# One core: six row tiles in one run per weight step of the first token group, and part of the third group's low parts on GpSimd

## The chip, the cores and the metric

The kernel runs on one core of a Trainium2 chip. The metric is the device time of one execution in microseconds (us), taken as the median of several executions. TensorE multiplies (PE in the profile; its weight loads are PEld), VectorE (DVE) and ScalarE (ACT) do elementwise work and read the matmul banks in PSUM, GpSimd (POOL) does elementwise work between SBUF tiles, and SyncE (SP) issues the DMAs.

## The reference, cut to what matters

Attention produces 2304 rows of 512 values; two expert layers follow. The change lies in the second, where every one of 8 experts multiplies all rows, and a gate `P` weighs the results:

```python
def _moe2_ref(x, w_gate, w1, w2):            # x: 2304 x 512
    P = np.exp(x @ w_gate - max)             # 2304 x 8
    for _ in range(8):
        P /= P.sum(1, keepdims=True) + 1e-09
        P /= P.sum(0, keepdims=True) + 1e-09
        P *= N / E
    out = np.zeros((N, D))
    for e in range(E):                       # 8 experts
        h = np.maximum(x @ w1[e], 0.0)       # 512 -> 1024
        ye = h @ w2[e]                       # 1024 -> 512
        out += P[:, e:e + 1] * ye
    return out
```

## The kernel before, in words

**Groups and steps.** The second expert layer takes the rows in three groups of 768, 768 and 640 (`g` = 0, 1, 2), and for each group the weights in 32 steps (`U2`; a step is 256 of an expert's 1024 hidden columns). Step `s` belongs to group `s // 32`. Every float32 operand is split into a high part, rounded for TensorE's fast float32 form, and a low part, the rest; a product is the three matmuls high x low, high x high and low x high.

**The first product of a step** (`quad`, line 908) multiplies 2 x 2 blocks by Winograd's scheme with seven block products `m1`, `m6`, `m5`, `m7`, `m2`, `m4`, `m3`, each six matmuls of 384 columns (320 in the third group), written to three banks `px`, `py` and `pz`. `m1` fills `px`, which ACT copies out as `p1`, and `m2` later adds to the same bank. `m6` fills `py`; DVE adds `p1` into `u2`; `m7` adds to `py`; DVE makes `u3` of it; `m4` adds to `py` again, and DVE makes `c21`. `m5` fills `pz`; with `u3` DVE makes `c22`; `m3` adds to `pz`, and with `u2` DVE makes `c12`. A product that adds to a bank waits until the reader of the bank's earlier state is through. ACT's rectified copies of `c11` (which is `px`), `c21`, `c22` and `c12` are the high parts `g2h`, and DVE makes the low parts `g2l` (line 975), which the list `later` puts off by a place or more.

**The second product of a step** is done, for group 0, one step later by `layer2_moe` (line 1267): six row tiles of 128 rows, each six matmuls of 512 columns into a bank `po` (three banks), which DVE adds, weighed by the gate, to `oa` (line 1303; an eviction below). For groups 1 and 2 it is seven products `pm` of the same scheme, six matmuls each, interleaved with those of the next step, and DVE adds each to `m` (line 1135).

**The order of the work** is written by hand. `experts()` goes through the steps and through seven places `i` of each step; at a place it issues the block product `mults[i]` and then, in group 0, the row tile `t` with `min(t + 1, 6) == i`. After each of them `slot()` lets every lane go one step on: lane `w` splits the next step's first weights (`weights_a`), `w2` this step's second weights (`weights_b`: ACT makes `w2h` as soon as the load `rw` has landed, GpSimd then `w2l`), and `sb` makes the sums of second weights which groups 1 and 2 will use (`sums_b`: two ACT copies and a cast, four DVE sums, two DVE low parts `wz`), stores them and starts the load of the next second weights. In six steps (`APART_AT`) lane `sb` makes a second set of sums, and in four (`SPREAD_AT`) it turns gate weights with TensorE transposes (`spread_p`). All engines run their instructions in the order in which they are written.

**Between groups** the right operands of the next group are made: `sums_of` and `form_now` (line 692) for the third group, where ACT makes a form's high part and DVE its low part in two halves, `T1`, `T3`, `B21`, `T4` and `B22` during steps 63 and 64 (lane `late`).

Of the kernel before, what the change touches and what calls it, by code (L numbers as in the profile page):

```python
# [84 lines left out]
def body(ctx: ExitStack, tc: tile.TileContext, xt_in, xn_in, stb, stk, wd, ws, alpha, wgate, out):  # L85
# [610 lines left out]
    def form_now(g, name, tag, src):  # L696

        t = big.tile([P, 2, 2, CH[2 * g][1]], F32R, tag=tag, name=f"r{name}_{g}")
        right[name, g] = t
        nc.scalar.activation(out=t[:, 0], in_=src, func=AF.Copy)  # L700
        yield 2
        for k in range(2):
            nc.vector.tensor_tensor(out=t[:, 1, k], in0=src[:, k], in1=f32(t[:, 0, k]), op=ALU.subtract)
            yield 1
# [222 lines left out]
    def quad(s):  # L927
# [81 lines left out]

        return [m1, m6, m5, m7, m2, m4, m3]  # L1010

# [336 lines left out]
    def slot():  # L1348
        tick()
        for lane in lanes:  # L1350
            if at_point.get(lane):
                continue
# [104 lines left out]

    APART_AT = [8, 11, 14, 16, 18, 20]
    SPREAD_AT = {22: (1, 0), 23: (1, 3), 24: (2, 0), 25: (2, 3)}

    def experts():
# [3 lines left out]
        for s in range(NS2 + 1):  # L1465
# [24 lines left out]

            lag = 3 if s == 1 else 1

            for i in range(7):
# [4 lines left out]
                if mults:  # L1498
                    point()
                    mults[i]()  # L1500
                    if made:
                        forms_in(made, after[i])
                    if i == 2 and s == 2 * U2 - 1:
                        lanes["late"].append(forms_late(2, after[2:]))
                    if i == 1:
                        while later:
                            later.pop(0)()
                    slot()
                for t in plain:
                    if min(t + lag, 6) == i:  # L1510
                        point()
                        layer2_moe(s - 1, t)
                        if t == 0 and UE < s < U2 - 1:
                            lanes["sb"].append(sums_own(s))
                            if s in APART_AT:
                                lanes["sb"].append(sums_apart(APART_AT.index(s)))
                            if s in SPREAD_AT:
                                lanes["sb"].append(spread_p(*SPREAD_AT[s]))
                        while later and i > 1:
                            later.pop(0)()  # L1520
                        slot()
                if U2 < s < NS2:
                    product(s - 1, i)
                    slot()
            for lane in ("w", "w2", "sums", "blocks"):
                flush(lane)
        flush("out")
        finish_last(NG - 1)
# [66 lines left out]
```

## Time and profile before

| | |
|---|---|
| median of 3 executions | 1772.21 us (1770.85 to 1772.26) |
| the profiled execution's own time | 1771.78 us |
| its span, first to last instruction | 1770.0 us |
| PE busy | 1751.9 us (99%) |
| DVE, ACT, POOL busy | 1418.4, 731.2, 1209.9 us |
| TensorE clock granted in the span | 0.999 of full speed |

The span is the stretch that the trace covers; the execution's own time is 1.78 us longer. PE's busy time counts a matmul from its start to a modelled end, and matmuls overlap, so the useful number for PE is the distance from one start to the next. Times in rows count from the span's start. The second expert layer's steps begin at 379.11 us; in group 0, step 20 begins at 698.65, step 28 at 825.07; step 64, the first of the third group, begins at 1354.80.

### The profile page before, as it was taken

What the parts mean: (1) busy time and instruction counts of PE and PEld (TensorE: products, weight loads), DVE (VectorE), ACT (ScalarE), POOL (GpSimd) and SP (SyncE); (2) the same over time, 40 slices, a digit from 0 to 9 for tenths busy, and PEclk for the clock granted to TensorE, in tenths of its full rate; (3) what the DMA queues carried; (4) which work ended last, traced back from release to release, by engine and by line L of the source; (5) the groups of instructions that cost most, each with busy time, mean ns of one, the idle gap of its engine ahead of it and who ended that gap; (6) DMA issues with size and microseconds to landing.
All of it is one profiled execution on the core that took longest, in us unless ns stands there. A gap on an engine that the chain in (4) does not pass through costs nothing.

```text
span 1770.0 us, 28923 instructions
## 1 busy us (share of the span) xinstructions
PE 1751.9 (99%) x9963; PEld 1635.7 (92%) x9963; DVE 1418.4 (80%) x2356; ACT 731.2 (41%) x1382; POOL 1209.9 (68%) x1288
## 2 busy tenths in 40 slices
PE   8999999999999999999999999999999999999998
PEld 8888888878888888888899999999999999999998
DVE  7879878788977788778877777777898777777877
ACT  7747757553344444444422222222233333322222
POOL 4536546577576766667657777777787897777775
PEclk9999999999999999999999999999999999999999
DMA  6212111227689999888876776777676887888884
GB/s 221 84 54 72 37 60 49 78 79 250 228 316 346 332 341 359 330 309 295 318 289 259 259 262 255 259 261 261 256 259 255 315 296 287 337 311 306 302 313 156
DMA packets 153010, 427.19 MB, mean 241 GB/s; under 512 B 17296, under 2 KB 34192, under 8 KB 152864
## 3 DMA queue, kind: packets, MB, share of 16 engines
q1 hardware_dynamic: 152864, 425.34, 66.4%
q8 instruction: 80, 1.31, 0.3%
q14 instruction: 66, 0.54, 0.1%
HBM read 302.28 MB, written 122.99 MB: 240 GB/s over the span
## 4 chain that ended last, share of the span: by engine, by line
PE 90%; DVE 5%; ACT 2%; POOL 1%; DMA 1%; issue 1%; SPq 0%; DVEq 0%; POOLq 0%; ACTq 0%
PE pm L1129 24%; PE py L950 16%; PE po L1279 15%; PE pz L950 11%; PE px L950 11%; PE po L626 8%; PE ph L594 4%; PE pv L520 1%; DVE acc L639 1%; PE psr L374 1%; PE pg L419 1%; DVE raw L165 0%; DVE al L533 0%; PE psc L296 0%; DVE r L602 0%
## 5 line engine op out<-in xcount | busy, mean ns | idle before, releaser
L1135 DVE TENSOR_TENSOR m<-pm,m 128x768 f32<-128x768 f32 (+1 forms) x427 | 378.6, 887 | 137.7 <-PE pm L1129 137.7
L1129 PE MATMUL pm<-formgh,wz 128*128 128x384 f32 (+1 forms) x1134 | 212.6, 322 | 0.4 <-POOL formgl L1066 0.4
L1056 POOL TENSOR_TENSOR formgh<-mid,formgh 128x384 fp32r<-128x384 f32 (+1 forms) x126 | 119.4, 948 | 117.8 <-ACT formgh L1055 117.7
L950 PE MATMUL py<-rT,wsh 128*128 128x384 f32 (+1 forms) x768 | 187.7, 326 | 0.6 <-DVE u L957 0.6
L950 PE MATMUL px<-rB,wah 128*128 128x384 f32 (+1 forms) x768 | 187.9, 327 | 0.0
L1129 PEld LDWEIGHTS pm<-formgh,wz 128*128 128x128 f32 x1134 | 186.7, 188 | 0.6 <-POOL formgl L1066 0.6
L769 POOL TENSOR_TENSOR w2l<-rw,w2h 128x512 fp32r<-128x512 f32 x64 | 82.4, 1311 | 150.1 <-ACT w2h L767 146.2
L1303 DVE SCALAR_TENSOR_TENSOR oa<-po,pr,oa 128x512 f32<-128x512 f32 x168 | 125.0, 744 | 48.2 <-PE po L1279 47.4
L1279 PE MATMUL po<-w2l,g2h 128*128 128x512 f32 x384 | 152.4, 397 | 0.0
L1279 PE MATMUL po<-w2h,g2h 128*128 128x512 f32 x384 | 151.6, 395 | 0.0
L1279 PE MATMUL po<-w2h,g2l 128*128 128x512 f32 x384 | 150.0, 391 | 0.0
L950 PEld LDWEIGHTS px<-rB,wah 128*128 128x128 f32 x768 | 136.1, 188 | 6.0 <-DVE g2l L975 0.3
L1055 ACT ACTIVATE formgh<-mid 128x384 fp32r<-128x384 f32 (+1 forms) x126 | 63.0, 500 | 189.6 <-DVE mid L1040 133.1
L950 PEld LDWEIGHTS py<-rT,wsh 128*128 128x128 f32 x768 | 135.6, 188 | 3.9 <-DVE u L957 1.0
L1066 POOL TENSOR_TENSOR T<-mid,mid 128x384 f32<-128x384 f32 (+1 forms) x126 | 117.3, 952 | 20.1 <-DVE mid L1040 20.1
L608 POOL TENSOR_TENSOR gl<-r,gh 128x512 fp32r<-128x512 f32 x64 | 88.0, 1385 | 58.3 <-ACT gh L112 36.6
L957 DVE TENSOR_TENSOR u<-py,p 128x384 f32<-128x384 f32 (+1 forms) x192 | 102.6, 534 | 30.6 <-PE py L950 22.5
L950 PE MATMUL px<-rB,wal 128*128 128x384 f32 (+1 forms) x384 | 125.2, 326 | 0.0
L950 PE MATMUL py<-rT,wsl 128*128 128x384 f32 (+1 forms) x384 | 125.1, 326 | 0.0
L1066 POOL TENSOR_TENSOR formgl<-T,formgl 128x384 fp32r<-128x384 f32 (+1 forms) x126 | 121.0, 960 | 1.1 <-ACT formgl L1073 0.7
L1129 PE MATMUL pm<-formgl,w2h 128*128 128x384 f32 (+1 forms) x504 | 120.8, 322 | 0.4 <-DVE m L1135 0.4
L1066 POOL TENSOR_TENSOR formgh<-T,formgh 128x384 fp32r<-128x384 f32 (+1 forms) x126 | 120.9, 959 | 0.0
(274 smaller groups left out, 4869.9 us busy)
## 6 DMA issues: line engine op xcount, KB each, us to landing
wz<-kept_bs SPq DMA_DIRECT2D x126, 512.0 KB, 8.2
kept_bs<-wz SPq DMA_DIRECT2D x64, 512.0 KB, 6.4
wsh<-kept_as_h SPq DMA_DIRECT2D x64, 512.0 KB, 3.7
wsl<-kept_as_l SPq DMA_DIRECT2D x64, 512.0 KB, 6.1
wah<-kept_a_h SPq DMA_DIRECT2D x64, 384.0 KB, 2.9
wal<-kept_a_l SPq DMA_DIRECT2D x64, 384.0 KB, 4.3
w2h<-kept_b_h SPq DMA_DIRECT2D x63, 384.0 KB, 6.7
w2l<-kept_b_l SPq DMA_DIRECT2D x63, 384.0 KB, 7.2
```

The lines of the kernel that those rows point to most:

```text
L594: nc.tensor.matmul(ps, lhsT=w, rhs=x, start=(i == 0), stop=(i == len(terms) - 1))
L608: nc.gpsimd.tensor_tensor(out=lo, in0=r, in1=f32(hi), op=ALU.subtract)
L626: nc.tensor.matmul(bank, lhsT=w, rhs=x, start=first_of, stop=last_of)
L769: nc.gpsimd.tensor_tensor(out=lo[:, i], in0=src[:, i], in1=f32(hi[:, i]), op=ALU.subtract)
L950: nc.tensor.matmul(bank[b], lhsT=w[:, k * P:(k + 1) * P], rhs=xf[:, j, k, :], start=(first and i == 0), stop=(i == 5), skip_group_check=True,)
L957: nc.vector.tensor_tensor(out=out, in0=bank[b], in1=t[x], op=ALU.add)
L1056: nc.gpsimd.tensor_tensor(out=lo, in0=out, in1=f32(hi), op=ALU.subtract)
L1066: nc.gpsimd.tensor_tensor(out=out, in0=x, in1=y, op=ALU.subtract)
L1129: nc.tensor.matmul(ps[:, q, :n], lhsT=w[:, q * P:(q + 1) * P], rhs=x, start=(j == 0), stop=(j == 2))
L1135: nc.vector.tensor_tensor(out=mm[g][name], in0=ps[:, :, :n], in1=mm[g][name], op=ALU.add)
L1279: nc.tensor.matmul(ps, lhsT=x[:, f, t * P:(t + 1) * P], rhs=w[:, f, :], start=(i == 0), stop=(i == 3 * NF - 1))
L1303: nc.vector.scalar_tensor_tensor(out=a, in0=ps, scalar=p, in1=a, op0=ALU.mult, op1=ALU.add)
```

## The change

**The run.** In the steps `s` with 9 < s < 31 that have no second set of sums (`in_a_run`: 11, 13, 15, 17, 19 and 21 to 30, fifteen of them) `quad` returns the block products as `m1`, `m6`, `m2`, `m7`, `m5`, `m4`, `m3`, and all six row tiles stand together at place 2, behind `m2`. `m7_first` makes `u3` from `py` alone, and `m5_then` makes `c22`. Each list `later` is emptied one place after it was filled. The step's own weight sums enter lane `sb` at the beginning of the step instead of behind the first row tile, and the lane is held from the last row tile to the end of the step.

**Other steps.** The second set of sums moves from steps 8, 11, 14, 16, 18, 20 to 10, 12, 14, 16, 18, 20, and the gate's transposes from steps 22 to 25 to 6 to 9.

**The third group's forms.** In `form_now` both low halves of `T1` and the second of `T3` go from DVE to GpSimd.

```diff
@@ form_now
         for k in range(2):
-            nc.vector.tensor_tensor(out=t[:, 1, k], in0=src[:, k], in1=f32(t[:, 0, k]), op=ALU.subtract)
+            eng = nc.gpsimd if name == "T1" or (name, k) == ("T3", 1) else nc.vector
+            eng.tensor_tensor(out=t[:, 1, k], in0=src[:, k], in1=f32(t[:, 0, k]), op=ALU.subtract)
@@ quad
-        return [m1, m6, m5, m7, m2, m4, m3]
+        def m7_first():
+            mult("y", "S3", "T3")
+            add(temp("u3", "u3", 1), "p1", "y")
+
+        def m5_then():
+            mult("z", "S1", "T1", True)
+            put("c22", "u3", "z")
+            relu(1, 1, "c22")
+
+        return [m1, m6, m2, m7_first, m5_then, m4, m3] if in_a_run(s) else [m1, m6, m5, m7, m2, m4, m3]
+
+    def in_a_run(s):
+        return 2 * UE + 1 < s < U2 - 1 and s not in APART_AT
@@ slot
-            if at_point.get(lane):
+            if at_point.get(lane) or lane in held:
@@
-    APART_AT = [8, 11, 14, 16, 18, 20]
-    SPREAD_AT = {22: (1, 0), 23: (1, 3), 24: (2, 0), 25: (2, 3)}
+    APART_AT = [10, 12, 14, 16, 18, 20]
+    SPREAD_AT = {6: (1, 0), 7: (1, 3), 8: (2, 0), 9: (2, 3)}
+    held = set()
+    def weight_sums(s):
+        lanes["sb"].append(sums_own(s))
+        if s in APART_AT:
+            lanes["sb"].append(sums_apart(APART_AT.index(s)))
+        if s in SPREAD_AT:
+            lanes["sb"].append(spread_p(*SPREAD_AT[s]))
@@ experts
+            run = in_a_run(s)
+            if run:
+                weight_sums(s)
...
                     point()
+                    due = list(later) if run else []
+                    if run:
+                        later.clear()
+                        (held.add if i > 2 else held.discard)("sb")
                     mults[i]()
+                    for fn in due:
+                        fn()
...
-                    if i == 1:
+                    if i == 1 and not run:
                         while later:
                             later.pop(0)()
                     slot()
                 for t in plain:
-                    if min(t + lag, 6) == i:
+                    if (2 if run else min(t + lag, 6)) == i:
                         point()
                         layer2_moe(s - 1, t)
-                        if t == 0 and UE < s < U2 - 1:
-                            lanes["sb"].append(sums_own(s))
...
+                        if t == 0 and UE < s < U2 - 1 and not run:
+                            weight_sums(s)
                         while later and i > 1:
                             later.pop(0)()
+                        if run and t == GT[0][1] - 1:
+                            held.add("sb")
                         slot()
...
+            held.clear()
```

Three places show how it moves instructions. In a name, the number behind it is the step (`px28`, `g2l27`), in `po2_27_0` the step whose rows it finishes and the tile.

The first is PE in step 28, from the end of `m6` on, before:

```order
L950 MATMUL py28_8961<-rT2_0_3639,wsh_28_8771 128x384 x2
L950 MATMUL py28_8961<-rT2_0_3639,wsl_28_8772 128x384
L1279 MATMUL po2_27_0_8978<-w2h_27_8776,g2l27_8755 128x512
L1279 MATMUL po2_27_0_8978<-w2h_27_8776,g2h27_8754 128x512
L1279 MATMUL po2_27_0_8978<-w2l_27_8777,g2h27_8754 128x512
L1279 MATMUL po2_27_0_8978<-w2h_27_8776,g2l27_8755 128x512
L1279 MATMUL po2_27_0_8978<-w2h_27_8776,g2h27_8754 128x512
L1279 MATMUL po2_27_0_8978<-w2l_27_8777,g2h27_8754 128x512
L950 MATMUL pz28_8989<-rT1_0_3516,wsh_28_8771 128x384 x2
L950 MATMUL pz28_8989<-rT1_0_3516,wsl_28_8772 128x384
L950 MATMUL pz28_8989<-rT1_0_3516,wsh_28_8771 128x384 x2
L950 MATMUL pz28_8989<-rT1_0_3516,wsl_28_8772 128x384
```

and PE in step 28 after, from the end of `m2` on:

```order
L951 MATMUL px28_8937<-rB21_0_3553,wah_28_8769 128x384 x2
L951 MATMUL px28_8937<-rB21_0_3553,wal_28_8770 128x384
L1292 MATMUL po2_27_0_8990<-w2h_27_8776,g2l27_8754 128x512
L1292 MATMUL po2_27_0_8990<-w2h_27_8776,g2h27_8753 128x512
L1292 MATMUL po2_27_0_8990<-w2l_27_8777,g2h27_8753 128x512
L1292 MATMUL po2_27_0_8990<-w2h_27_8776,g2l27_8754 128x512
L1292 MATMUL po2_27_0_8990<-w2h_27_8776,g2h27_8753 128x512
L1292 MATMUL po2_27_0_8990<-w2l_27_8777,g2h27_8753 128x512
L1292 MATMUL po2_27_1_9006<-w2h_27_8776,g2l27_8754 128x512
L1292 MATMUL po2_27_1_9006<-w2h_27_8776,g2h27_8753 128x512
L1292 MATMUL po2_27_1_9006<-w2l_27_8777,g2h27_8753 128x512
L1292 MATMUL po2_27_1_9006<-w2h_27_8776,g2l27_8754 128x512
```

Where row tiles of 512 columns and block products of 384 columns took turns, the second row tile now follows the first; four more stand behind, then `m7`, `m5`, `m4`, `m3` without a tile between them.

The second is DVE in the latter part of step 28 before (`sumx` and `wz` are the weight sums, `sxh4_1` a sum for the second group's right operands):

```order
L894 TENSOR_TENSOR sumx_28_8986<-rw2_28_8872,sumy_28_8987 128x256
L898 TENSOR_TENSOR wz_28_0_9037<-sumy_28_8987,wz_28_0_9037 128x512
L1303 SCALAR_TENSOR_TENSOR oa0_4065<-po2_27_3_9062,pr_96,oa0_4065 128x512
L975 SCALAR_TENSOR_TENSOR g2l28_8937<-px28_8938,g2h28_8936 128x384
L898 TENSOR_TENSOR wz_28_1_9038<-sumx_28_8986,wz_28_1_9038 128x512
L957 TENSOR_TENSOR c21_28_9081<-py28_8961,p1_28_8945 128x384
L1303 SCALAR_TENSOR_TENSOR oa0_4065<-po2_27_4_9084,pr_96,oa0_4065 128x512
L975 SCALAR_TENSOR_TENSOR g2l28_8937<-c21_28_9081,g2h28_8936 128x384
L957 TENSOR_TENSOR c12_28_9099<-pz28_8989,u2_28_8968 128x384
L691 TENSOR_TENSOR sxh4_1_8766<-acc1_767 128x384
L1303 SCALAR_TENSOR_TENSOR oa0_4065<-po2_27_5_9104,pr_96,oa0_4065 128x512
L975 SCALAR_TENSOR_TENSOR g2l28_8937<-c12_28_9099,g2h28_8936 128x384
```

and DVE from the fourth eviction of step 28 on, after:

```order
L1316 SCALAR_TENSOR_TENSOR oa0_4065<-po2_27_3_9044,pr_96,oa0_4065 128x512
L899 TENSOR_TENSOR wz_28_1_9004<-sumx_28_8961,wz_28_1_9004 128x512
L1316 SCALAR_TENSOR_TENSOR oa0_4065<-po2_27_4_9054,pr_96,oa0_4065 128x512
L1316 SCALAR_TENSOR_TENSOR oa0_4065<-po2_27_5_9062,pr_96,oa0_4065 128x512
L958 TENSOR_TENSOR u3_28_9078<-py28_8964,p1_28_8944 128x384
L958 TENSOR_TENSOR c22_28_9088<-pz28_9081,u3_28_9078 128x384
L958 TENSOR_TENSOR c21_28_9098<-py28_8964,p1_28_8944 128x384
L976 SCALAR_TENSOR_TENSOR g2l28_8936<-c22_28_9088,g2h28_8935 128x384
L691 TENSOR_TENSOR sxh4_1_8766<-acc1_767 128x384
L958 TENSOR_TENSOR c12_28_9109<-pz28_9081,u2_28_8971 128x384
L976 SCALAR_TENSOR_TENSOR g2l28_8936<-c21_28_9098,g2h28_8935 128x384
L976 SCALAR_TENSOR_TENSOR g2l28_8936<-c12_28_9109,g2h28_8935 128x384
```

The evictions and the weight sums stand together ahead of `u3`; behind it only the step's own sums and low parts are left, and in this step a sum for the second group, between `g2l` of `c22` and `c12`.

The third is POOL in step 63 before (`formgh`, `formgl` are the second group's forms for the products `pm`):

```order
L1066 TENSOR_TENSOR formgh1_9797<-T2_62_14459,formgh1_9797 128x384
L1066 TENSOR_TENSOR formgl1_9798<-T4_62_14472,formgl1_9798 128x384
L1056 TENSOR_TENSOR formgh0_9696<-mid63_0_14512,formgh0_9696 128x384 x2
L1056 TENSOR_TENSOR formgl0_9735<-mid63_1_14553,formgl0_9735 128x384
L1066 TENSOR_TENSOR T3_63_14611<-mid63_0_14512,mid63_1_14553 128x384
L1066 TENSOR_TENSOR T1_63_14613<-mid63_1_14553,mid63_0_14512 128x384
L1066 TENSOR_TENSOR formgl0_9735<-T3_63_14611,formgl0_9735 128x384
L1066 TENSOR_TENSOR T2_63_14626<-mid63_0_14512,T1_63_14613 128x384
```

and POOL there after:

```order
L1079 TENSOR_TENSOR formgh1_9797<-T2_62_14459,formgh1_9797 128x384
L1079 TENSOR_TENSOR formgl1_9798<-T4_62_14472,formgl1_9798 128x384
L1069 TENSOR_TENSOR formgh0_9696<-mid63_0_14512,formgh0_9696 128x384
L704 TENSOR_TENSOR rT1_2_14491<-acc2_1283,rT1_2_14491 128x320 x2
L1069 TENSOR_TENSOR formgh0_9696<-mid63_0_14512,formgh0_9696 128x384
L1069 TENSOR_TENSOR formgl0_9735<-mid63_1_14553,formgl0_9735 128x384
L704 TENSOR_TENSOR rT3_2_14536<-acc2_1283,rT3_2_14536 128x320
L1079 TENSOR_TENSOR T3_63_14611<-mid63_0_14512,mid63_1_14553 128x384
L1079 TENSOR_TENSOR T1_63_14613<-mid63_1_14553,mid63_0_14512 128x384
L1079 TENSOR_TENSOR formgl0_9735<-T3_63_14611,formgl0_9735 128x384
```

Three low halves of the third group's forms stand between the second group's; on DVE they stood here before:

```order
L1040 SCALAR_TENSOR_TENSOR mid63_0_14512<-mid63_0_14512,pb_9540 128x384
L703 TENSOR_TENSOR rT1_2_14491<-acc2_1283,rT1_2_14491 128x320
L1135 TENSOR_TENSOR m3_1_9804<-pm62_3_14518,m3_1_9804 128x768
L703 TENSOR_TENSOR rT1_2_14491<-acc2_1283,rT1_2_14491 128x320
L1040 SCALAR_TENSOR_TENSOR mid63_0_14512<-px63_14420,pb_9540 128x384
L1135 TENSOR_TENSOR m3_1_9804<-pm62_4_14538,m3_1_9804 128x768
L957 TENSOR_TENSOR py63_14461<-py63_14461,p1_63_14427 128x384
L1040 SCALAR_TENSOR_TENSOR mid63_1_14553<-py63_14461,pb_9540 128x384
L703 TENSOR_TENSOR rT3_2_14536<-acc2_1283,rT3_2_14536 128x320
L1135 TENSOR_TENSOR m3_1_9804<-pm62_5_14558,m3_1_9804 128x768
L703 TENSOR_TENSOR rT3_2_14536<-acc2_1283,rT3_2_14536 128x320
```

The rows `rT1` and the second of `rT3` are gone from DVE after, and nothing else moves there.

## Rows read from the trace of the kernel before

**Rows 1.** Windows: stretch, length, busy time and count by engine, clock, DMA share, GB/s.

```profile
1619.58:1631.90 12.32, 12.32 (x86) 12.32 (x85) 9.68 (x17) 3.64 (x8) 9.38 (x12) 1.00 0.81 298
698.65:714.29 15.64, 15.64 (x80) 14.06 (x79) 11.47 (x22) 7.38 (x13) 10.61 (x13) 1.00 0.98 356
1340.24:1354.80 14.56, 14.56 (x85) 14.56 (x85) 11.45 (x18) 5.54 (x11) 9.91 (x12) 1.00 0.76 275
1354.80:1370.55 15.75, 14.35 (x85) 13.50 (x85) 15.47 (x24) 5.74 (x11) 11.88 (x12) 1.00 0.65 236
```

**Rows 2.** Timeline of step 20: start, length (us), engine, line, operation, out<-in, count [idle before].

```profile
698.32 0.55 DVE L957 TENSOR_TENSOR c<-pz,u 128x384 f32<-128x384 f32 x1
...
698.90 0.53 ACT L974 ACTIVATE g2h<-c 128x384 fp32r<-128x384 f32 x1 [1.66 <-DVE c L957]
...
699.69 0.51 PE L950 MATMUL py<-rT,wsh 128*128 128x384 f32 x2
...
699.89 0.49 ACT L981 ACTIVATE p<-px 128x384 f32<-128x384 f32 x1 [0.47 <-PE px L950]
...
700.73 0.39 PE L1279 MATMUL po<-w2h,g2l 128*128 128x512 f32 x1
...
701.00 0.56 DVE L957 TENSOR_TENSOR u<-py,p 128x384 f32<-128x384 f32 x1 [0.93 <-PE py L950]
...
702.12 0.51 PE L950 MATMUL pz<-rT,wsh 128*128 128x384 f32 x2
```

**Rows 3.** Timeline of PE near the kernel's end, five row tiles in a run.

```profile
1755.10 0.39 PE L1224 MATMUL pe<-w2h,g2xh 128*128 128x512 f32 x1
...
1756.49 0.39 PE L1224 MATMUL pe<-w2h,g2xh 128*128 128x512 f32 x1
...
1760.57 0.39 PE L1224 MATMUL pe<-w2h,g2xh 128*128 128x512 f32 x1
...
1761.94 0.82 PE L1232 MATMUL pt<-ident,blocks 128*128 128x128 f32 x6
```

**Rows 4.** DVE's groups in steps 26 to 30: count | busy us, mean ns | idle before.

```profile
L1303 DVE SCALAR_TENSOR_TENSOR oa<-po,pr,oa 128x512 f32<-128x512 f32 x30 | 22.3, 743 | 10.4 <-PE po L1279 10.4
...
L691 DVE TENSOR_TENSOR sxl<-acc,sxl 128x384 f32<-128x384 f32 x4 | 3.5, 870 | 0.0
L898 DVE TENSOR_TENSOR wz<-sumy,wz 128x512 fp32r<-128x512 f32 x5 | 3.4, 677 | 0.0
```

**Rows 5.** Timeline of ACT in step 22, the cast of the second weights.

```profile
733.11 1.06 ACT L767 ACTIVATE w2h<-rw 128x1024 fp32r<-128x1024 f32 x1 [1.44 <-DMA rw<-in_ws_dram]
```

**Rows 6.** Timeline of steps 63 and 64, all engines.

```profile
1349.45 0.48 DVE L703 TENSOR_TENSOR rT<-acc,rT 128x320 fp32r<-128x320 f32 x1
...
1350.25 1.01 POOL L1056 TENSOR_TENSOR formgh<-mid,formgh 128x384 fp32r<-128x384 f32 x1 [1.76 <-ACT formgh L1055]
...
1350.72 0.89 DVE L703 TENSOR_TENSOR rT<-acc,rT 128x320 fp32r<-128x320 f32 x1
...
1355.26 0.88 DVE L703 TENSOR_TENSOR rT<-acc,rT 128x320 fp32r<-128x320 f32 x1
...
1357.13 0.95 DVE L1135 TENSOR_TENSOR m<-pm,m 128x768 f32<-128x768 f32 x1
...
1358.22 0.59 PE L1129 MATMUL pm<-formgl,w2h 128*128 128x384 f32 x2 [0.45 <-DVE m L1135]
...
1364.40 1.17 DVE L1040 SCALAR_TENSOR_TENSOR mid<-mid,pb 128x320 f32<-128x320 f32 x1
...
1365.49 0.94 DVE L1135 TENSOR_TENSOR m<-pm,m 128x768 f32<-128x768 f32 x1
...
1366.58 1.28 PE L1129 MATMUL pm<-formgh,wz 128*128 128x384 f32 x6 [0.39 <-POOL formgl L1066]
...
1368.41 0.47 DVE L703 TENSOR_TENSOR rB<-acc,rB 128x320 fp32r<-128x320 f32 x1
...
1368.94 0.56 PE L950 MATMUL pz<-rB,wsh 128*128 128x320 f32 x2 [0.57 <-DVE rB L703]
```

More of the change, by code (lines that the diff above doesn't have):

```diff
@@ L1509, in experts @@
                 for t in plain:
-                    if min(t + lag, 6) == i:
+                    if (2 if run else min(t + lag, 6)) == i:
                         point()
                         layer2_moe(s - 1, t)
-                        if t == 0 and UE < s < U2 - 1:
-                            lanes["sb"].append(sums_own(s))
[L1515 to L1518, printed above, removed]
+                        if t == 0 and UE < s < U2 - 1 and not run:
+                            weight_sums(s)
                         while later and i > 1:
                             later.pop(0)()
+                        if run and t == GT[0][1] - 1:
+                            held.add("sb")
                         slot()
```

## The prediction

> **What bounds the kernel now.** I read the windows of whole steps first, then the timeline of one step, then the groups of DVE, then the timeline where the third group begins. In a step of the first group PE is busy for the whole 15.64 us of its length at full clock [rows 1]: it waits for nobody there, and only a smaller distance between matmuls can shorten the step. DVE is busy for 11.47 of the 15.64, ACT for 7.38, POOL for 10.61 [rows 1]: there is room, but every block product has a reader that must be in time. Step 64 is another case: 15.75 us long with PE busy for 14.35, while DVE is busy for 15.47 [rows 1]. There PE loses 1.40 us, in three waits of 0.45, 0.39 and 0.57 [rows 6], and DVE is the late one. So the change has two parts to cost: PE's spacing in the first group, and DVE's load ahead of step 64. The profiled execution took 1771.78 us, 0.43 below the median of 1772.21; the sum is made against 1771.78.
>
> **Part one, the run: what a row tile costs alone.** Step 63 has no row tiles: its 14 products are 84 matmuls of 384 columns in 14.56 us [rows 1], so one takes 14.56 / 84 = 0.1733 us, and the 42 of a step's block products take 7.28. A row tile between two block products takes from 700.73 to 702.12, which is 1.39 us [rows 2]. Together 7.28 + 6 x 1.39 = 15.62, against 15.64 measured: nothing is missing from this account.
>
> **What it costs in a run.** The trace of before has such a run near its end [rows 3], with other operands but the same shapes: the first tile takes 1756.49 - 1755.10 = 1.39, the middle ones (1760.57 - 1756.49) / 3 = 1.36, the last 1761.94 - 1760.57 = 1.37. Six in a run are then 1.39 + 4 x 1.36 + 1.37 = 8.20 where six alone are 8.34, a gain of 0.14 us per step; against the measured 15.64 the step becomes 7.28 + 8.20 = 15.48, a gain of 0.16. I take 0.15 for each of 15 steps: 2.2 us (2.1 to 2.4). It is a small gain, since only the change between the two shapes is saved.
>
> The Trainium skill, "TensorE: Matmul & The Clock Gate", section on the back-to-back issue gap, gives a matmul's distance as N / 2.4 + 2.5 ns, from its own column count alone; by that rule no order saves anything. The trace disagrees: the same six matmuls take 1.39 or 1.36 us by what stands beside them [rows 2, 3].
>
> **What the run takes away.** Between a product and the one that needs its result a row tile used to lie, 1.39 us beside the 1.04 of a product (6 x 0.1733). Behind the run `m7`, `m5`, `m4`, `m3` stand bare, and `m4` needs `u3`, made from `m7`, with only `m5` between. The chain: DVE starts 701.00 - 700.73 = 0.27 after the next matmul group has begun, works 0.56 [rows 2], and PE goes on 0.06 after a DVE operation's end (1368.94 against 1368.41 + 0.47) [rows 6]. That is 0.89 against 1.04: it fits with 0.15 to spare, if DVE is free. The same holds for `m5`, `c22`, `m3`. At the step's start `m1`, `m6`, `m2` stand bare too, and `m2` needs `p1`. ACT's copy of `c12` stands ahead of `p1`: `c12` ends 0.27 + 0.55 = 0.82 after `m3`'s end, ACT follows 0.03 later for 0.53, so at 1.38; `p1` takes 0.49, to 1.87 [rows 2]; PE could go on at 1.93 against 2.08 for two products. Again 0.15 to spare.
>
> **Whether DVE is free.** In the run each tile of 1.36 us asks DVE for an eviction of 0.743 and a weight sum or low part of up to 0.677 [rows 4], 1.42 in the worst pairing, 0.06 per tile too much, which three or four such pairings make 0.2; then the lane is held, so that no sum follows the last eviction. The last eviction ends 0.27 + 0.74 = 1.01 behind the run, and `m7` ends at 1.04, so `u3` is asked for at 1.31: 0.3 to spare, 0.1 after such a backlog. I therefore cost these edits at nothing; the cover is the 0.15 and the 0.3, and if it is gone each late operation shows in PE at once, which is the slower rival below.
>
> **Two places where I do charge.** In step 28 a sum for the second group stands between the low part of `c22` and `c12` (the order of DVE above). From `c21`'s start DVE works 0.55, a low part taken at the same 0.55, and the sum of 0.87 [rows 4], 1.97 in all, while `m3` is through after 1.04. `c12` comes 0.93 late, and the next step's `m2` up to 0.93 - 0.15 = 0.8 late; with the sum at 0.48, the shortest such operation of the trace [rows 6], 0.4. If the low part comes before `c21` it is less. I take 0.5. The second is the load of the second weights: in step 22 ACT stood 1.44 us waiting for it [rows 5], with a row tile's grace that hid it. In the run the low half is needed early. Bounds: nothing, or 1.44 once; I take 0.2, since PE lost nothing there before. The second sets of sums and the gate's transposes only move between steps of the same kind; their instructions are as many as before, and steps 6 to 9 are bound by PE like the others, so they pay there what steps 22 to 25 saved: 0.
>
> **Part two, the third group's low parts.** DVE loses three operations of 0.48, 0.89 and 0.88 [rows 6], 2.25 us, all ahead of step 64's first wait. POOL gets them. A form on POOL takes 1.01 for 384 columns [rows 6]; these have 320, so about 0.85 each, and POOL is busy for 9.91 of 14.56 in step 63 and 11.88 of 15.75 in step 64 [rows 1], so three more fit. The first wait, 0.45 for DVE's `m` that starts at 1357.13, stands 2.25 us of queue behind and goes. The second, 0.39, names POOL's form, but DVE's `m` ends at 1365.49 + 0.94 = 1366.43, just ahead of the matmul at 1366.58, and one DVE operation before it took 1.17 [rows 6]. In between DVE will have caught up and wait for PE, so that a lead of 2.25 at the start is worth less here. The third, 0.57 for `rB` at 1368.41, stands at the end of the same queue. What can be had at most: step 64 has 42 matmuls like step 63's, 7.28, less 42 of 320 columns: the third group's 84 matmuls in 12.32 [rows 1] are 0.1467 each, 6.16, so 13.44 in all and 2.3 below 15.75. What is sure is about the first wait, 0.5. I take 1.1, the first wait and about half of the other two with the spacing around them (0.5 to 2.0).
>
> The move does not remove a collision that the rows show: a low part on DVE took 0.48 alone and 0.89 in the stretch in which POOL's form of 1.01 ran [rows 6]. The Trainium skill, "SBUF — State Buffer", section on who interferes with whom, says that a DVE instruction with two SBUF inputs and a GpSimd instruction that reads SBUF block each other fully. The rows agree (0.48 against 0.89). By it each moved operation can hold up a DVE operation for some 0.4 us, 3 x 0.4 = 1.2 us given back of 2.25, which speaks against this part.
>
> **The sum.** 1771.78 - 2.2 + 0.5 + 0.2 - 1.1 = 1769.2 us, 0.17% below the median of before. A difference of 0.2%, 3.5 us, is about what a measurement of this kernel can tell from no change, so the bounds are 1768.7 and 1775.8.
>
> **The rivals.**
> *All goes well.* No stall is added, and step 64 loses nearly all its waits: 1771.78 - 2.4 - 2.0 = 1767.4. For it: 0.15 is left at each tight place, and DVE gets 2.25 us of lead. Against: the queue's catching up, and step 28. Chance 0.23.
> *DVE or ACT late behind the run* (the slower side). Each run step has three places with 0.15 to spare, and DVE operations beside POOL take up to 0.4 longer (0.89 against 0.48) [rows 6]; one such stretch at `u3`, or in front of `c12`, costs PE 0.25. The gains are 3.3 in all, so from 3.3 / 15 = 0.22 us per run step the kernel is no faster. Two late places per step, 0.5, give 1771.78 - 3.3 + 15 x 0.5 = 1776.0. For it: POOL works 10.61 of 15.64 us. Against: the operations at those places read a bank of PSUM, and the weight sums are kept away from them. Chance 0.15, of which 0.08 beyond +0.2%.
> *The third group gains nothing*, since the collisions eat it or the second and third wait grow: 1771.78 - 2.2 + 0.7 = 1770.3. For it: the second wait's row names POOL, which gets more work. Chance 0.12.
> *The run gains nothing*, because PE's distance follows from the column count alone: 1771.78 + 0.7 - 1.1 = 1771.4. Against it: 1.36 and 1.39 in the rows, though from another place of the program. Chance 0.05.
> That the change does not do what it says is excluded by the orders shown.
>
> **How the numbers follow.** The forecast, 1769.2, has 0.45, the rivals 0.23, 0.15, 0.12 and 0.05. The forecast's own range, by its terms' bounds, is 1768.0 to 1770.6. Faster by over 0.2% (below 1768.7) is the first rival, 0.23, and a third of the forecast, 0.15, together 0.38; slower by over 0.2% is the outer half of the second, 0.08; the rest, 0.54, is within 0.2%. The range reaches from the lower side of the first rival, 1767.0, to 1772.4, which takes in both cases of a part without gain and a run with 0.2 lost per step.
>
> **What would show it.** Right: run steps of 15.48 to 15.50 with PE busy throughout, row tiles 1.36 apart, step 64 near 14.6 with the first wait gone, steps 6 to 9 longer and 22 to 25 shorter by the same. Wrong: PE idle ahead of `m4` or `m3` with DVE as releaser, or ahead of `m2` with ACT, in many run steps; or a step 64 as long as before. A loss of over 0.22 us at these places in most run steps makes the prediction wrong.

## The result, and the profile after

The changed kernel takes 1786.3 us (median of 5 executions, 1785.2 to 1791.0) against 1772.1 for the kernel before: a ratio of 1.0087, with a 95% interval of 1.0076 to 1.0098. It is slower by 14 us; the forecast was 1769.2, and the range ended at 1772.4. The profiled execution took 1786.23 us with a span of 1784.5, which is 14.5 us over the span before.

The windows of whole steps show where they went. Columns as in [rows 1]: stretch, length, busy time and count of PE, PEld, DVE, ACT and POOL, granted clock, DMA share, GB/s. The stretches are step 13, a part of it, step 25 and step 64:

```profile
590.43:610.01 19.58, 17.59 (x79) 15.25 (x78) 15.25 (x29) 7.96 (x15) 10.28 (x13) 0.91 0.93 353
594.90:599.00 4.10, 4.10 (x13) 3.55 (x13) 2.50 (x5) 3.50 (x6) 3.13 (x3) 0.58 0.52 148
794.48:809.99 15.51, 15.51 (x80) 14.07 (x80) 11.89 (x22) 6.70 (x13) 10.30 (x13) 1.00 0.85 302
1370.55:1385.31 14.76, 14.14 (x86) 13.50 (x85) 14.48 (x23) 5.22 (x10) 12.10 (x12) 1.00 0.66 248
```

Step 25 is a run step as it was meant: 15.51 against 15.64 [rows 1], with PE busy throughout. Step 64 fell from 15.75 to 14.76. Step 13, a run step too, takes 19.58. By the distances between the first matmuls of the steps, the account is (the steps that are not listed change by 0.05 at most):

| steps | change, us |
|---|---|
| 13, 15, 17, 19, 21 (run, each behind a step with a second set of sums) | +15.7 (19.58, 18.21, 19.72, 18.45, 17.95; before 15.64 each) |
| 23 (run, had transposes before) | +0.6 |
| 22, 24, 25 (run, had transposes before) | -1.3 |
| 11, 26, 27, 28, 30 (run) | -0.7 |
| 6 to 9 (the transposes now) | +1.3 |
| 64 | -1.0 |
| sum | +14.6 |

So nine of the fifteen run steps, the moved transposes and the third group went nearly as forecast, five steps cost 3 us each, and step 23, at 16.58, took 1.07 more than a run step as it was meant. What PE and ACT wait for from step 11 to step 21 says which engine is late (columns: engine, line, waited for, us in total, times, longest):

```profile
PE px L951 <- ACT p L982: 10.0, 5, 2.0
PE py L951 <- DVE c L958: 0.9, 3, 0.4
...
ACT wz L902 <- DMA kept_bs<-wz: 19.4, 5, 4.2
ACT w2h L768 <- DMA rw<-in_ws_dram: 1.1, 2, 0.6
```

Five times PE stands some 2 us ahead of `m2`, waiting for ACT's `p1`, and five times ACT stands some 4 us in front of a cast for the weight sums, waiting until the tile `wz` that it will overwrite has been stored to DRAM. In these steps of the kernel before, PE waits for nobody and ACT for no store. The timeline around the start of step 13 (at 590.43) joins the two; columns as in [rows 2]:

```profile
589.67 0.60 ACT L902 ACTIVATE wz<-sumx 128x512 fp32r<-128x512 f32 x1 [3.56 <-DMA kept_bs<-wz]
...
590.30 0.69 DVE L899 TENSOR_TENSOR wz<-sumx,wz 128x512 fp32r<-128x512 f32 x1 [2.26 <-ACT wz L902]
...
590.91 0.55 DVE L958 TENSOR_TENSOR c<-py,p 128x384 f32<-128x384 f32 x1
...
591.37 0.74 DVE L1316 SCALAR_TENSOR_TENSOR oa<-po,pr,oa 128x512 f32<-128x512 f32 x1
...
591.49 0.53 ACT L975 ACTIVATE g2h<-c 128x384 fp32r<-128x384 f32 x1 [1.22 <-DVE c L958]
...
592.04 0.56 DVE L976 SCALAR_TENSOR_TENSOR g2l<-c,g2h 128x384 fp32r<-128x384 f32 x1
...
592.54 0.43 DVE L887 TENSOR_TENSOR sumy<-sumx,rwl 128x256 f32<-128x256 f32 x1
...
592.88 0.55 DVE L958 TENSOR_TENSOR c<-pz,u 128x384 f32<-128x384 f32 x1
...
593.46 0.52 ACT L975 ACTIVATE g2h<-c 128x384 fp32r<-128x384 f32 x1 [0.95 <-DVE c L958]
...
593.89 0.58 ACT L893 ACTIVATE wz<-sumy 128x512 fp32r<-128x512 f32 x1
...
594.37 0.48 ACT L982 ACTIVATE p<-px 128x384 f32<-128x384 f32 x1
...
594.90 0.44 PE L951 MATMUL px<-rB,wah 128*128 128x384 f32 x1 [1.99 <-ACT p L982]
```

Read it from the top. Of the lane's three ACT operations per set, one is a copy (line 885) and two are casts into `wz` (lines 893 and 902). The second cast of step 12's own sums starts after 3.56 us of waiting. DVE's low part `wz` waits for it, and `c21` (`c<-py`) stands behind that low part in DVE's order, so it comes at 590.91. An eviction, a low part and a sum of the second set stand behind it, and `c12` (`c<-pz`), which without a queue would start about 0.3 us into step 13, starts at 592.88. ACT's copy of `c12` and a cast for the second set stand ahead of `p1`, which ends at 594.85, 4.42 us into the step. PE goes on with `m2` at 594.90.

The store that the cast waits for is that of the second half of step 11's sums. Before, it was issued at 571.18, 13.3 us into step 11; after, at 584.41, 9.6 us into step 12:

```profile
571.18 0.32 SPq L780 DMA_DIRECT2D kept_bs<-wz  x1
```

```profile
584.41 0.45 SPq L781 DMA_DIRECT2D kept_bs<-wz  x1
```

(the first is before, the second after, both from the timeline of SP's queue). The same cast before, in step 12, waited 0.78 us, and for a sum:

```profile
585.06 0.60 ACT L901 ACTIVATE wz<-sumx 128x512 fp32r<-128x512 f32 x1 [0.78 <-DVE sumx L894]
```

It is the issue that is late and not the transfer: in the stretch from 557 to 747 us these stores take 7.0 us (median) from issue to landing before, and 5.5 after. In step 11 the lane of the weight sums first finishes the second set of step 10; its own sums begin after that, the run leaves the lane few places, and the hold stops it behind the fourth sum. So both low parts and both stores slide into the next step, which has its own; DVE makes the low parts 1.1 and 3.8 us into step 12. The load of the next second weights, issued behind the fourth sum, comes 10.4 us into step 11 where it came at 8.8.

### The profile page after: what moved, and what is told of

Read it like the earlier page. It is cut to its first block, busy times and chain, and to the rows that moved or that the text cites. A ratio compares the mean times of both kernels' runs of the same rounds, so it can differ in the third digit from the quotient of the medians.

```text
span 1784.5 us, 28937 instructions
## 1 busy us (share of the span) xinstructions
PE 1755.3 (98%) x9963; PEld 1637.2 (92%) x9963; DVE 1425.3 (80%) x2353; ACT 729.9 (41%) x1382; POOL 1209.4 (68%) x1291
## 4 chain that ended last, share of the span: by engine, by line
PE 56%; POOL 3%; DMA 3%; issue 1%; DVE 1%; ACT 0%; SPq 0%; DVEq 0%; POOLq 0%; ACTq 0%
PE pm L1142 23%; PE py L951 12%; PE pz L951 8%; PE px L951 8%; PE po L1292 5%; DMA rw<-in_ws_dram 2%; POOL w2l L770 1%; POOL wal L770 1%; DMA kept_as_h<-wsh 1%; POOL wsl L770 0%; PE pe L1237 0%; POOL sum L803 0%; POOL sum L806 0%; DVE m L1148 0%; DMA kept_bs<-wz 0%
```

## The experiments

Theory S (store): the late store blocks ACT's cast, and through the orders of ACT and DVE `c12` and `p1`. Rival Q (queue): `p1` is late because the second set's cast and sums stand ahead of it, whatever the store does.

**e1, the second part alone.** The kernel before with the two changed lines of `form_now`.

> The kernel before with the second part alone: the three low halves of the third group's forms on GpSimd. Step 64 took 15.75 us before and 14.76 in the changed kernel. If the parts are independent, step 64 falls by 0.9 to 1.1 here too and no other step changes: 1771.0 us against 1772.1. If the gain in the changed kernel came from its other timing, step 64 stays above 15.4 and the time at 1771.8 or more.

Measured: 1770.9 us against 1772.0, ratio 0.9993 (0.9984 to 1.0003); the profiled execution 1770.79 against 1771.78. Step 64 takes 14.77 as in the changed kernel, and the only wait of PE left in it is the third one:

```profile
PE pz L951 <- DVE rB L704: 0.6, 1, 0.6
```

Before, this row stood beside two of 0.4 [rows 6]. The two parts are independent, and this one is worth 1.0 us, which the medians can't tell from no change and the step's length can.

**e2, a second buffer.** Odd steps put the second half of their sums into another tile:

```diff
-        homes = (p2["z"], "z"), (big, "xl3" if u < U2 - 6 else "xh5")
+        homes = (p2["z"], "z"), (big, "xl3" if u < U2 - 6 and u % 2 == 0 else "xh5")
```

> The changed kernel with a second buffer for the second half of the weight sums, used in turn by odd and even steps; nothing else is moved. Theory S (store): in steps 12, 14, 16, 18, 20 and 22 ACT's cast waits 3.6 to 4.3 us for the store of the sums of the step before, which the hold has pushed into this step, and the copies of c21, c12 and p1 queue behind it; with a buffer free that wait is gone, the steps 13, 15, 17, 19 and 21 fall from 18 to 20 us to 15.5 to 15.7, and the time is 1769 to 1770.5. Rival Q (queue): p1 is late because the cast of the second set and DVE's sums for it stand ahead of it in the order; they still do, so these steps stay at 17 us or more and the time at 1782 or more.

**e3, no hold in the steps behind a second set.**

```diff
-                        (held.add if i > 2 else held.discard)("sb")
+                        (held.add if i > 2 and s - 1 not in APART_AT else held.discard)("sb")
...
-                        if run and t == GT[0][1] - 1:
+                        if run and t == GT[0][1] - 1 and s - 1 not in APART_AT:
```

> The changed kernel with the lane of the weight sums not held in steps 11, 13, 15, 17, 19 and 21, which follow a second set of sums; their sums and stores then end in the step itself, and ACT's order around p1 stays as it is. Theory S: the store lands before the next step's cast, ACT does not wait for it, the steps take 15.5 to 15.7, and the time is 1769 to 1770.5; where sums now stand at u3 or c22, up to 0.5 us per step may come on top (1773). Rival Q: the second set's cast still stands ahead of p1, 1782 or more.

Measured: e2 1773.3 us, ratio 1.0007 (0.9998 to 1.0017); e3 1771.4 us, 0.9996 (0.9987 to 1.0005). Q falls: 13 to 15 us are back though the second set's cast stands ahead of `p1` as before. S holds for most of it, but both kernels miss its number by 1 to 3 us, and the lengths of the steps and the ends of `p1` show where (us; a step from its first matmul to the next step's first; `p1` from its step's first matmul to the end of the copy; PE comes in time while `p1` ends by about 2.0, two products of 1.04 less the 0.05 that PE takes to go on):

| step | before | after | e2 | e3 | e4 | e5 | e7 | e9 | e10 |
|---|---|---|---|---|---|---|---|---|---|
| 13, length | 15.64 | 19.58 | 15.58 | 15.61 | 15.67 | 17.50 | 15.64 | 15.63 | 17.73 |
| 15, length | 15.64 | 18.21 | 16.43 | 16.40 | 15.64 | 17.50 | 15.64 | 15.63 | 19.89 |
| 17, length | 15.64 | 19.72 | 16.98 | 16.08 | 15.85 | 17.50 | 15.64 | 15.63 | 17.64 |
| 19, length | 15.64 | 18.45 | 16.62 | 16.01 | 15.68 | 17.52 | 15.64 | 15.63 | 21.36 |
| 21, length | 15.64 | 17.95 | 15.90 | 16.18 | 15.64 | 17.50 | 15.64 | 15.63 | 19.70 |
| 22, length | 15.97 | 15.51 | 15.59 | 15.51 | 17.18 | 16.87 | 15.51 | 15.51 | 15.51 |
| 13, `p1` | 1.74 | 4.42 | 1.97 | 1.80 | 4.24 | 3.91 | 1.73 | 1.79 | 4.13 |
| 15, `p1` | 1.74 | 4.62 | 2.82 | 2.68 | 4.00 | 3.91 | 1.88 | 1.79 | 4.86 |
| 17, `p1` | 2.05 | 4.82 | 3.38 | 2.35 | 4.40 | 3.91 | 2.60 | 1.79 | 4.04 |
| 22, `p1` | 1.74 | 1.73 | 1.73 | 1.73 | 3.40 | 2.20 | 1.73 | 1.73 | 1.73 |

In e3 step 13 is whole and steps 15 to 21 are not. Most of what is left lies in ACT's waits for loads from step 11 to 22, of e2 (first row) and e3 (e3 has one wait for a store, 2.0 us in step 22, a step that takes 15.51):

```profile
ACT w2h L768 <- DMA rw<-in_ws_dram: 5.5, 5, 1.8
```

```profile
ACT w2h L768 <- DMA rw<-in_ws_dram: 3.8, 5, 1.1
```

The load of the second weights is issued behind the last read of the sums before; sums that come late make it late. In e3 `p1` is late by about 0.8 of the wait in the step before, step by step (the numbers stand in what was expected of e9). That was the new theory L (load), beside S. e9 and e10 test it, below.

Step 23, which the account above leaves at 16.58, has its own part of this. PE waits there ahead of `m4` for `u3`, the other place that the prediction's slower rival named:

```profile
PE py L951 <- DVE u L958: 0.7, 1, 0.7
```

With the hold of step 21, that step's low parts come in step 22, and the last of step 22's in step 23, where DVE's sums and low parts then stand late ahead of `u3`. In e2, without any wait for a store, step 23 still takes 16.31; in e3 and e9, without the hold in step 21, it takes 15.51. So there it is the hold that counts, and not the store's wait.

**e4, the run in ten steps.**

```diff
-        return 2 * UE + 1 < s < U2 - 1 and s not in APART_AT
+        return 2 * UE + 1 < s < U2 - 1 and s not in APART_AT and (s < 12 or s - 1 not in APART_AT)
```

> The changed kernel with the run in ten steps only: 11 and 22 to 30; the five steps 13, 15, 17, 19 and 21, in which p1 was late, keep the old order of products. Both theories: these five steps return to 15.64, so 15.7 us less the 5 x 0.13 that they had not gained, and step 23, which came late after the held step 21, to 15.5: 1786.3 - 15.7 - 0.7 = 1769.9. Theory S beside it: in step 12, behind the held step 11, ACT's cast still waits 3 to 4 us for the store, and step 13 loses nothing by it, since four row tiles stand ahead of its m2. If something else in the changed kernel is slow, the time stays above 1772.

Measured: 1773.6 us, ratio 1.0007 (0.9997 to 1.0016), above the bound named. The five steps are back to 15.64 to 15.85, as expected, and they show what the old order forgave. In step 13 ACT's queue is as late as in the changed kernel (the cast of step 12 waited 3.6 us for the store), `p1` ends 4.24 us into the step, and PE loses nothing: `m2` is its fifth product, with three row tiles ahead of it (not four, as the expectation has it), and starts 8.37 us into the step. The timeline of ACT, step 13 from 590.49:

```profile
593.30 0.53 ACT L975 ACTIVATE g2h<-c 128x384 fp32r<-128x384 f32 x1 [0.95 <-DVE c L958]
593.74 0.58 ACT L893 ACTIVATE wz<-sumy 128x512 fp32r<-128x512 f32 x1
594.21 0.48 ACT L982 ACTIVATE p<-px 128x384 f32<-128x384 f32 x1
```

```profile
590.49:606.16 15.67, 15.67 (x80) 14.01 (x79) 13.49 (x28) 8.09 (x15) 10.28 (x13) 1.00 0.90 336
731.95:749.13 17.18, 15.97 (x80) 14.00 (x78) 13.28 (x25) 7.13 (x13) 10.47 (x14) 1.00 0.91 317
```

(windows of steps 13 and 22). But the lateness stays: `p1` ends at 3.4 to 4.4 in every step from 13 to 22, and step 22, the first run again, pays 1.67 us for it (17.18 against 15.51). I had not expected that one held step, the 11th, could do this eleven steps later; that it is this step, e7 shows.

**e5 and e6, `p1` ahead of the second set's sums.** As e3, with the lane also held at the end of a step that has a second set, so that the cast comes behind `p1` (e6: from one place earlier, `i == 5`):

```diff
+                if i == 6 and s in APART_AT:
+                    held.add("sb")
```

> As e3_no_hold_behind_second_set, and the lane of the weight sums is also held from the last product of a step that has a second set (10, 12, ... 20), so that the second set's cast comes behind p1 in ACT's order and one DVE sum fewer stands ahead of u2. In e3 five steps still lost 0.1 to 0.9 us against 15.51, 2.7 us in all, p1 ending 1.80 to 2.68 us into its step where 1.73 is its time without a queue. If that rest is the cast (0.58) and the sum it waits for, p1 ends at 1.73 to 2.0 in all five steps, they take 15.5 to 15.6, and the time is 1769.0 to 1769.8 where e3 had 1771.4. If the rest comes from DVE's evictions and low parts ahead of c12, p1 stays late and the time within 0.5 us of e3; if sums that now stand at u3 and c22 are late instead, PE waits move from m2 to m4 and m3 and the time is 1771 or more.

> As e5_p1_ahead_of_sums, but the hold in the steps with a second set begins one place earlier: neither of DVE's first two sums of the second set stands ahead of c12 or p1, and in return the sums of the run step are made and stored later, the last store again in the following step. Theory: p1 ends at 1.73 in all five steps, but the sums stand at u3, c22 and c12 of the run step (up to 0.4 us each), and the late store is waited for by ACT's cast in the even steps, 1 to 2 us; with old order there nothing is lost, and the next step's p1 decides: 1769 to 1770 if c12 and p1 are in time, 1772 to 1776 if the store's wait reaches them.

Measured: 1787.0 us, ratio 1.0084 (1.0071 to 1.0098), and 1790.9 us, 1.0107 (1.0093 to 1.0120): 15.6 and 19.5 us worse than e3, far outside what I had written. The cast does stand behind `p1`, and `p1` ends at 3.91. The rows of e5 for steps 11 to 21 show two places where PE waits:

```profile
PE px L951 <- DVE g2l L976: 7.3, 4, 3.1
PE px L951 <- ACT p L982: 6.1, 4, 1.5
...
ACT w2h L768 <- DMA rw<-in_ws_dram: 18.3, 5, 4.3
```

What the lane doesn't do at the end of step 10 it does in step 11, so step 11's own sums come later and with them the load for step 12. ACT's cast of these weights waits 2.52 us in step 12, GpSimd's sums for the next step stand behind the same operations, ACT waits for those (4.36 us, no longer than the 4.69 in e3, but ending 2.8 us later in the step), and `c21`, `c12` and `p1` are late by another way:

```profile
578.15 1.06 ACT L768 ACTIVATE w2h<-rw 128x1024 fp32r<-128x1024 f32 x1 [2.52 <-DMA rw<-in_ws_dram]
...
585.35 0.63 ACT L768 ACTIVATE wsh<-sum 128x512 fp32r<-128x512 f32 x1 [4.36 <-POOL sum L806]
585.89 0.51 ACT L975 ACTIVATE g2h<-c 128x384 fp32r<-128x384 f32 x1
```

(ACT's timeline in step 12 of e5.) The larger row is not ahead of `m2`. It stands at the start of steps 15, 17, 19 and 21, where `m1` waits for DVE's low part `g2l` that reads `px` of the step before:

```profile
623.94 0.44 PE L951 MATMUL px<-rB,wah 128*128 128x384 f32 x1 [1.40 <-DVE g2l L976]
```

So the steps with a second set, 15.64 in e3, lengthen too: steps 14, 16, 18 and 20 take 17.20, 17.57, 19.04 and 16.84. Less work ahead of `p1` made `p1` later: what counted was when that work ended, and what waited for it. In e6 PE's waits under the same two names are 6.8 and 6.1 us, and 3.3 us more are for DVE's `u`; what makes e6 worse than e5 stays open.

**e7 and e8, the run only behind the last second set.** e7 has it in steps 22 to 30; e8 moves the second sets to 8, 10, ... 18 and has it in 20 to 30.

```diff
-        return 2 * UE + 1 < s < U2 - 1 and s not in APART_AT
+        return APART_AT[-1] + 1 < s < U2 - 1
```

> The changed kernel with the run only in steps 22 to 30, all of them behind the last second set (step 20); steps 11 to 21 keep the old order and no lane is held there. Against e4_ten_runs only step 11 differs. Backlog theory: the lane of the weight sums is one queue; a held or short step behind a second set pushes its sums, its stores and the next load of second weights into the following step, and each following second set keeps them late. Without the run in step 11 p1 ends at 1.73 to 2.1 us in all steps 12 to 22 (3.4 to 4.4 in e4), no wait is left in steps 16, 17 and 22 (2.1 us in e4), nine steps take 15.51, and with step 64 the time is 1.2 + 1.0 below before: 1769.8. If the late p1 of e4 had its cause in the moved second sets (10, 12, 14) alone, p1 stays late in 12 to 21 and step 22 loses 1 to 1.5 us: 1771.

> As e7_nine_runs, with the second sets in steps 8, 10, 12, 14, 16 and 18, and the run in steps 20 to 30. Two more steps gain 0.13 each: 1769.5. The risk: a second set in step 8 shares the lane with the gate's transposes of steps 8 and 9, and a backlog from there to step 19 would show as p1 over 2.0 us in step 20 and a loss there of up to 1.5 us.

Measured: e7 1771.1 us, ratio 0.9995 (0.9986 to 1.0004), the profiled execution 1769.53 (the number given, 1769.8, is met by this execution and missed by the median by 1.3); e8 1775.3 us, 1.0020 (1.0011 to 1.0029). Against e4, e7 differs in step 11 alone, and the wait in step 22 is gone, as the backlog theory had it; its steps 11 to 21 take 15.64, steps 22 to 30 15.51 (29: 15.65). `p1` ends at 2.60 in step 17 and at 2.19 in step 19, above the 2.1 that I gave, without a cost in the old order. In e8 the risk came true: steps 11 and 12 take 16.56 and 18.68, `p1` is at 3.5 to 4.4 from step 11 to step 20, and step 20, a run, loses 1.6 us. That this comes from the second set of step 8, which shares the lane with the transposes, is argued from the order; the two were not tried apart.

**e9, an early load.** As e3, with the load of the second weights for the even steps 12 to 22 issued at the start of the step before, into a tile that is free there:

```diff
+    EARLY = range(12, 24, 2)
...
-        t = pool.tile([P, NF, DM], F32, tag="raw", name=f"rw2_{s}")
+        if s in EARLY:
+            t = big.tile([P, NF, DM], F32, tag="xh5", name=f"rw2_{s}")
+        else:
+            t = pool.tile([P, NF, DM], F32, tag="raw", name=f"rw2_{s}")
...
-        if s in APART:
+        if s in APART or s + 1 in EARLY:
             load_b2(s + 1, p2["raw"])
```

> As e3_no_hold_behind_second_set (fifteen runs), with the load of the second weights for the even steps 12 to 22 issued at the start of the step before, into a tile of its own, and not behind the weight sums. In e3 ACT waited for this load 0.00, 1.09, 0.77, 0.72 and 0.87 us in steps 12, 14, 16, 18 and 20, and p1 of the next step ended at 1.80, 2.68, 2.35, 2.32 and 2.47 us: late by about 0.8 of the wait. If that is the cause of the rest, ACT waits for none of these loads, p1 ends at 1.80 or earlier in steps 13 to 21, these steps take 15.5 to 15.65 as step 13 did, and the time is 1771.4 - 2.0 = 1769.4. If the rest comes from the second set's cast and sums in the queues (the queue theory), p1 stays at 2.3 to 2.7 and the time at 1771.4.

**e10, the early load with the hold.** The changed kernel with that edit alone.

> The changed kernel with the early load of e9_early_load alone; the lane is held as in the changed kernel and the second half of the sums has one buffer. If the store of the sums is the larger cause and the load the smaller one, ACT's cast still waits 3.5 to 4.3 us for the store in the even steps, p1 still ends at 4 us or later in steps 13, 15, 17, 19 and 21, each loses 2 us or more, and the time is 1782 to 1787. If the late load is the root of both, the time is 1769 to 1771 as in e9.

Measured: e9 1769.7 us, ratio 0.9986 (0.9977 to 0.9995), the profiled execution 1769.48. ACT waits for no load and no store in steps 11 to 21, `p1` ends at 1.79 in all of 13, 15, 17, 19 and 21, and each takes 15.63. It has the lowest ratio of the kernels here, 0.14% below the kernel before, with all fifteen runs; its interval overlaps with those of e1, e3 and e7. The windows of steps 13 and 15, and ACT at the start of step 15 (621.77):

```profile
621.77:637.40 15.63, 15.63 (x79) 14.00 (x78) 13.64 (x26) 7.47 (x14) 10.30 (x13) 1.00 1.02 384
590.50:606.13 15.63, 15.63 (x79) 14.00 (x78) 13.65 (x26) 7.46 (x14) 10.30 (x13) 1.00 0.98 375
```

```profile
622.17 0.53 ACT L979 ACTIVATE g2h<-c 128x384 fp32r<-128x384 f32 x1 [0.95 <-DVE c L962]
622.60 0.58 ACT L897 ACTIVATE wz<-sumy 128x512 fp32r<-128x512 f32 x1
623.08 0.48 ACT L986 ACTIVATE p<-px 128x384 f32<-128x384 f32 x1
```

The second set's cast still stands between the copy of `c12` and `p1`. With everything in time it costs `p1` 0.06 us (1.79 against 1.73) and PE nothing: the last word on Q. e10: 1784.6 us, ratio 1.0068 (1.0050 to 1.0086). With the hold the store's wait is back in full,

```profile
ACT wz L906 <- DMA kept_bs<-wz: 19.6, 5, 4.5
```

and the five steps lose 2.0 to 5.7 us each against 15.64. So both causes are real; the early load without the other change leaves the wait for the store as it was. The store behind the hold is the large one: freeing it brought 12.4 of the 16.4 us that the five steps of the changed kernel lose against 15.51 (e2) or, with fewer late loads, 13.6 (e3). The late load is the rest: of the 2.7 us left in e3, 2.1 went with it (e9), and the last 0.6, 0.12 per step, are sums that stand in DVE's order at the end of the unheld run steps (argued from that order, not tried).

## Why the prediction was wrong

**The run's gain** was right in mechanism and a little large. In step 25 the six row tiles take from 797.60 to the start of `m7` at 805.80, 8.20 in all, the sum that was forecast (PE's timeline; the first tile 1.39, the last 1.36):

```profile
797.60 0.39 PE L1292 MATMUL po<-w2h,g2l 128*128 128x512 f32 x1
...
798.99 0.39 PE L1292 MATMUL po<-w2h,g2l 128*128 128x512 f32 x1
...
804.44 0.39 PE L1292 MATMUL po<-w2h,g2l 128*128 128x512 f32 x1
...
805.80 0.51 PE L951 MATMUL py<-rT,wsh 128*128 128x384 f32 x2
```

The step is 15.51, so 0.13 per step and not 0.15; the block products take 7.31. The rival "the run gains nothing" falls. The Trainium skill, "TensorE: Matmul & The Clock Gate", section on the back-to-back issue gap, gives the formula that the prediction cites for an isolated matmul, and says that in a kernel the weight loads count too. No run here tries the weight loads apart.

**The third group** went as forecast: 0.99 for 1.1. Of the three waits two went and the third, 0.56, stayed, so nearly all of the gain lies in the first two, where I had given part of it to the third. Of the 1.2 us that the prediction works out as given back to collisions of DVE and GpSimd, 0.77 is seen. The low part of `T3` that stays on DVE takes 1.25 where it took 0.48: two of the moved operations now stand ahead of GpSimd's `formgh`, which ended at 1353.79 before and now runs beside it (DVE before, DVE after, GpSimd after):

```profile
1353.99 0.48 DVE L703 TENSOR_TENSOR rT<-acc,rT 128x320 fp32r<-128x320 f32 x1
```

```profile
1368.77 1.25 DVE L704 TENSOR_TENSOR rT<-acc,rT 128x320 fp32r<-128x320 f32 x1
```

```profile
1368.65 1.02 POOL L1069 TENSOR_TENSOR formgh<-mid,formgh 128x384 fp32r<-128x384 f32 x1
```

The trace agrees here with the Trainium skill, "SBUF — State Buffer", section on who interferes with whom, where a DVE instruction with two SBUF inputs contends with a GpSimd instruction that reads SBUF. DVE keeps a lead of about 1.5 of the 2.25 us, and step 64 gains 0.99 of it.

**The transposes** cost steps 6 to 9 1.3 us and gave it back in 22 to 25, as forecast, 0. **Step 28's sum** was charged 0.5 and cost 0.15 (step 29, 15.66). The **spare time of `p1`** was 0.3 and not 0.15: it ends at 1.73 where I had worked out 1.87, since ACT's operations overlap a little in the rows. The **own range of the forecast**, 1768.0 to 1770.6, does not come out of its terms: with the load of the second weights between nothing and 1.44 and step 28 between 0.4 and 0.8 it is 1767.8 to 1771.4. This had no part in the miss.

**The step that failed** is in "What the run takes away" and in "Two places where I do charge". I took the time of `p1` from one step without a queue (step 20) and wrote that ACT's copy of `c12` stands ahead of it. In five of the fifteen run steps a second set's sums end there, and I let that go with "only move between steps of the same kind; their instructions are as many as before": 0. They were as many, but the steps behind them were no longer of the same kind. These steps had the old order before; as runs they have fewer places for the lane and hold it at the end, and the lane's last acts are a store whose tile the next step overwrites, and, ahead of it, the load for the next step. I followed the lane's operations on DVE and never asked when its DMAs are issued, which the order of SP told: before, the store of step 11's second half stood ahead of step 12's stores of `w2h`; after, ten DMAs that are issued in step 12 stand ahead of it, the store of the first half among them.

The late load I did see, in [rows 5], and priced at 0.2 for step 22, where it cost nothing. The same load was at stake in the steps ahead of it; in e3, with the store out of the way, it made 2.1 us.

**The slower rival** named the side and one right place: PE ahead of `m2` with ACT as releaser. Its price was one late operation of 0.25 to 0.5 us in each of 15 steps. What came was a chain through the orders of ACT and DVE, 2 us of PE's waiting in each of five steps, and in two of them 1.1 to 1.8 us more at a lower clock. A margin of 0.15 or 0.3 us was the wrong thing to weigh: the lateness that arrived was ten times that.

## What to carry to other kernels

When a step is made tighter, look for its latest inputs in the steps where they are latest, not in a typical one: here the timeline of one quiet step stood for fifteen, and five had another queue ahead. A lane that is shortened or held keeps its work but moves its stores and loads; ask for each when the tile it frees is written next and who reads what it loads, and follow the waiting engine's order from there. Such a backlog need not go away by itself: in e4, with a second set in every second step, it was carried over eleven steps for 0.7 us in all, until a step without cover came.

## What the runs showed of the hardware

After PE had stood for 1.99 us ahead of `m2` in step 13, the granted clock was 0.58 on average in the 4.1 us that followed (the second window of the first fence), part of them at the lower of its two levels, 1.2 GHz, and the rest at 2.4 GHz. A window inside them shows the lower level alone:

```profile
596.00:598.50 2.50, 2.50 (x8) 2.11 (x7) 1.50 (x3) 2.40 (x5) 2.50 (x3) 0.50 0.44 75
```

There matmuls of 512 columns started 0.43 us apart where they take 0.23 at full clock. In step 17 it was the same; in steps 15, 19 and 21, after waits of 1.99 to 2.01 us, the clock stayed at full (1.00 over each of these steps; windows of steps 15 and 17):

```profile
625.65:643.86 18.21, 16.03 (x80) 13.97 (x79) 15.29 (x29) 7.90 (x16) 10.31 (x13) 1.00 0.92 327
659.49:679.21 19.72, 17.36 (x79) 15.21 (x78) 15.38 (x29) 8.33 (x16) 10.29 (x13) 0.91 0.88 324
```

Steps 13 and 17 are the longer ones by 1.1 to 1.8 us, and in e10 it was steps 15, 19 and 21 (granted clock 0.91, 0.84 and 0.91 over these steps). What decides between the two was not tried.
